# Eight stores of W2's raw blocks, issued 7 to 25 steps sooner

## The chip, the core and the metric

The kernel runs on one core of one Trainium2 chip. The metric is the time of one execution in microseconds on the device. A profiled execution gives, beside its own time, a span: first to last instruction of the core.

## What is computed

Grouped-query attention over 8 batches (16 query heads, 4 key and value heads, 384 tokens, head width 64) is followed by a ResMLP block with per-channel scales. In the reference's words, cut to what matters:

```python
attn = softmax(q @ k.T / sqrt(64));  x = heads side by side of (attn @ v)   # 8 x 384 x 1024
a1 = alpha1 * x + beta1
u  = x + lam * einsum('ts,bsd->btd', w_tok, a1)
a2 = alpha2 * u + beta2
out = u + lam * (np.maximum(a2 @ w_ch1, 0.0) @ w_ch2)    # w_ch1 1024 x 4096, w_ch2 4096 x 1024
```

The change lies in the last product, with `w_ch2`, called W2 from here.

## The kernel before

The batches are worked in four pairs. For each pair there are two large products: the first makes the hidden layer from `w_ch1`, the second multiplies it by W2. Both are done with a fast 2 x 2 scheme of seven half-size products, so that W2 is used as seven operand matrices, numbered 1 to 7: raw quarters of W2 (1, 2 and 3), and differences of quarters (4 to 7). Each operand matrix is kept as four blocks `c` of 512 KB in bfloat16.

The first pair is special. It reads W2's raw quarters from the input (float32, turned to bfloat16 on the way by transfers that GpSimd starts, L491), uses them, builds the differences with VectorE in `sum_w2` (L499), and stores each of the 28 blocks to a scratch tensor in HBM, `w2s`, with `keep_w2` (L494, started by SyncE). The other three pairs only read `w2s` back (`fetch`, L528). The blocks of one quarter carry its name: "11" lies at fixed places in the tile `arena` since the first product, "21", "12" and "22" pass through six slots of 512 KB in a ring (tile `w1`, called `w` in the profile) and three slots in the tile `pad`. "again" is the quarter "21" read a second time from `w2s` (L489).

The second product of the first pair, `second_product`, is a generator. It runs 21 turns of 16 matmuls of 128x128 by 128x512 (L752) and yields after every four, so that it has 84 steps, 0 to 83. Its turns are, as (operand, block of tokens): (1,0), (1,1), (2,0), (2,1), (1,2), (5,0), (2,2), (5,1), (5,2), then three each for operands 3, 6, 7 and 4. Operand 3 begins with step 36: its four blocks "22" 0 to 3 are read in steps 36, 37, 38 and 39.

When a slot comes free, `free` calls `pump`, which starts the next entry of one list, `queue`. The loads of "22" stand there behind those of "12": block 0 goes to `pad` at once, blocks 1 to 3 go to slots that operand 2 frees in its last turn, steps 24 to 27. The next entries are the four "again" blocks, then the blocks of `w_ch1` for the second pair (`load_w1`, L183).

Into the yields of both products other work is put by a table written out by hand, `plan`: what `put(pair, product, step, ...)` names is emitted just after that step. In the first pair's second product these are, besides the work on W2, the attention of batches 2 and 3 (`side(2)` at steps 0 to 39, `side(3)` 38 steps later): scores (L260), exponentials (L269), the product with v (L295), normalising (L303), the token product (L324 and L328), and for each pair of heads `p` a store of the sum (L227, SyncE) and a transpose by a transfer (L337, SyncE). Transposing transfers of q and k for batch 3 (L174, L170, SyncE) stand at steps 8, 14, 27, 32 and 33.

Each engine takes its instructions in the order of emission. SyncE's are nearly all starts of transfers, and in the built program each waits, beside its data, for the landing of the transfer that stands eight before it on that engine. The sums of heads lie in a pool of four buffers (`xr`) and the inputs of L337 in five places of `obuf`, so that a late store or transpose holds the buffer for the pair of heads four or five later.

Of the kernel before, what the change touches and what calls it, by code (L numbers as in the profile page):

```python
# [13 lines left out]
def kernel(  # L14
# [932 lines left out]
    with tc.manual_schedule(engines=order):  # L947
# [123 lines left out]
        def put(ps, phase, at, *m):  # L1071
            plan.setdefault((ps, phase, at), []).append(m)
# [25 lines left out]
        for c in range(4):  # L1098
            put(0, 0, (50, 72, 74, 44)[c], load_w2, "11", c)
            put(0, 0, (6, 14, 42, 46)[c], cast_w2, "21", c)  # L1100
            put(0, 1, (41, 43, 45, 47)[c], keep_w2, 1, c)
            put(0, 1, 38 + 2 * c, keep_w2, 3, c)
            put(0, 1, (9, 10, 13, 15)[c], sum_w2, 5, c)
            put(0, 1, (20, 21, 25, 26)[c], sums_first_hid, 2, c)
            put(0, 1, (28, 30, 31, 34)[c], sums_first_hid, 4, c)
            put(0, 1, (37, 40, 41, 43)[c], sum_w2, 6, c)
            put(0, 1, (44, 45, 49, 50)[c], sums_first_hid, 3, c)
            put(0, 1, (51, 54, 57, 58)[c], sum_w2, 7, c)
            put(0, 1, (61, 64, 68, 71)[c], last_w2, c)
        for u, o in ((77, 5), (79, 7), (81, 6)):  # L1110
            put(0, 1, u, sum_w1, 0, o)
        for ps in range(NB - 1):
            c = 2 * ps + 2
# [100 lines left out]
```

## Time and profile before

| | |
|---|---|
| median of 3 runs | 732.74 us (732.49 to 738.95) |
| the profiled execution's own time | 731.92 us |
| its span | 729.9 us |
| TensorE busy | 717.4 us, 98% |
| VectorE, ScalarE, GpSimd busy | 75%, 51%, 27% |
| granted TensorE clock | 1.000 |
| second product of the first pair | from 128.1 to about 234.3 us of the span |

The engines are called PE (TensorE), DVE (VectorE), ACT (ScalarE), POOL (GpSimd) and SP (SyncE) in the profile; q0 is the queue of the transfers that POOL starts, q1 that of SP's. An engine's busy time is only worth something where the end waits for that engine, so the stretch around the change is read by itself.

### The profile page before, as it was taken

To read this page: it belongs to the slowest core of one execution; us is meant where nothing else is said; L and a number is where in the kernel's file an instruction comes from. 1 tells how busy PE (TensorE), PEld (TensorE's weight loads), DVE (VectorE), ACT (ScalarE), POOL (GpSimd) and SP (SyncE) were. 2 spreads that over 40 slices of the span, in tenths; PEclk is the share of its full clock that TensorE was granted. 3 is DMA by queue.
4 is the path that set the end of the run, shared out by engine and by line. 5 is a ranking of instruction groups with operands and counts; after the bars stand their busy time and mean duration, and the time that the engine had idled before them with its cause. 6 is when DMAs were issued, how large, how long until landed. Compare 5 with 4: busy or idle time off the path is not lost.

```text
span 729.9 us, 14511 instructions
## 1 busy us (share of the span) xinstructions
PE 717.4 (98%) x5716; PEld 408.7 (56%) x5716; DVE 543.9 (75%) x1009; ACT 373.8 (51%) x566; POOL 199.2 (27%) x242
## 2 busy tenths in 40 slices
PE   8899999999999999999999999999999999999998
PEld 4665555555555666555555566655555566654444
DVE  7888876577888988649678888748868988763354
ACT  7877666544563666643433466663333366650000
POOL 8844233221046551201022344200002222000011
PEclk9999999999999999999999999999999999999999
DMA  9999999999999999969989999998989999937965
GB/s 164 180 239 231 190 195 227 226 242 235 366 312 232 179 182 196 234 221 207 272 193 220 160 162 194 212 227 201 270 233 183 210 126 146 165 123 264 302 174 104
DMA packets 197616, 153.26 MB, mean 210 GB/s; under 512 B 90540, under 2 KB 175892, under 8 KB 197292
## 3 DMA queue, kind: packets, MB, share of 16 engines
q0 software_dynamic: 109872, 64.47, 65.4%
q1 hardware_dynamic: 86988, 87.42, 42.8%
q8 instruction: 44, 0.72, 0.4%
q10 hardware_dynamic: 688, 0.46, 0.2%
q14 instruction: 24, 0.20, 0.1%
HBM read 155.23 MB, written 39.85 MB: 267 GB/s over the span
## 4 chain that ended last, share of the span: by engine, by line
PE 90%; DVE 4%; POOL 2%; DMA 1%; issue 1%; ACT 1%; DVEq 0%; ACTq 0%; POOLq 0%
PE C L897 30%; PE X L831 17%; PE C L752 10%; PE Y L831 9%; PE Z L831 4%; PE sc L260 4%; PE X L681 4%; PE sc L295 3%; PE sc L324 3%; PE Y L681 3%; DMA ops<-obuf 1%; DVE pad L565 1%; PE Z L681 1%; PE tok L324 1%; POOL obuf L334 0%
## 5 line engine op out<-in xcount | busy, mean ns | idle before, releaser
L897 PE MATMUL C<-w,arena 128*128 128x512 bf16 (+2 forms) x744 | 168.3, 372 | 0.0
L269 ACT ACTIVATE es<-sc 128x1024 bf16<-128x1024 f32 x108 | 104.1, 1024 | 116.0 <-PE sc L260 107.6
L897 PEld LDWEIGHTS <-arena 128*128 128x128 bf16 x1040 | 94.8, 98 | 100.5 <-issue 5.1
L442 POOL DMA_DIRECT2D out_dram<-hT x45 | 40.0, 888 | 294.7 <-DVE hT L790 135.9
L836 ACT ACTIVATE hT<-X,bias 128x384 f32<-128x384 f32 x144 | 83.6, 582 | 60.0 <-PE X L831 55.2
L831 PEld LDWEIGHTS <-w 128*128 128x128 bf16 x768 | 75.1, 98 | 50.0
L831 PEld LDWEIGHTS <-pad 128*128 128x128 bf16 x576 | 56.4, 98 | 37.2
L183 POOL DMA_DIRECT2D w<-in_moe_w_ch_dram x48 | 45.4, 1002 | 105.6 <-PE X L831 36.5
L831 PE MATMUL X<-ops,w 128*128 128x384 bf16 x384 | 70.3, 326 | 0.0
L831 PE MATMUL X<-ops,pad 128*128 128x384 bf16 x384 | 70.3, 326 | 0.0
L897 PE MATMUL C<-pad,arena 128*128 128x512 bf16 (+2 forms) x296 | 70.2, 373 | 0.0
L324 PEld LDWEIGHTS <-wtokT 128*128 128x128 bf16 x576 | 39.0, 98 | 16.4 <-issue 3.4
L752 PEld LDWEIGHTS <-arena 128*128 128x128 bf16 x336 | 29.8, 98 | 30.0 <-issue 2.5
L331 DVE TENSOR_TENSOR xr<-sc,xr 128x384 f32<-128x384 f32 x48 | 26.5, 553 | 25.6 <-PE sc L324 14.3
L752 PE MATMUL C<-w,arena 128*128 128x512 bf16 x168 | 41.2, 379 | 0.0
L838 DVE TENSOR_TENSOR arena<-Y,hT 128x384 bf16<-128x384 f32 x48 | 26.5, 556 | 17.7 <-ACT hT L836 16.0
L295 PEld LDWEIGHTS <-es 128*128 128x128 bf16 x864 | 32.8, 97 | 11.3
L831 PE MATMUL Y<-ops,w 128*128 128x384 bf16 x192 | 39.1, 326 | 0.0
L831 PE MATMUL Z<-ops,w 128*128 128x384 bf16 x192 | 39.0, 326 | 0.0
L269 ACT ACTIVATE hT<-sc 128x1024 bf16<-128x1024 f32 x36 | 35.8, 1031 | 4.3 <-PE sc L260 4.0
L260 PE MATMUL sc<-qT,kT 64*128 64x384 bf16 (+2 forms) x504 | 37.2, 271 | 0.5 <-ACT hT L269 0.2
L842 ACT ACTIVATE arena<-X,bias 128x384 bf16<-128x384 f32 x48 | 27.9, 582 | 17.7 <-PE X L831 16.1
(190 smaller groups left out, 1175.1 us busy)
## 6 DMA issues: line engine op xcount, KB each, us to landing
w<-w2s SPq DMA_DIRECT2D x67, 512.0 KB, 5.1
w<-in_moe_w_ch_dram POOLq DMA_DIRECT2D x65, 512.0 KB, 9.8
pad<-w2s SPq DMA_DIRECT2D x25, 512.0 KB, 6.9
out_dram<-hT POOLq DMA_DIRECT2D x45, 256.0 KB, 7.1
out_dram<-xr SPq DMA_DIRECT2D x48, 192.0 KB, 5.3
q_raw<-in_q_dram POOLq DMA_DIRECT2D x28, 192.0 KB, 9.5
w2s<-w SPq DMA_DIRECT2D x10, 512.0 KB, 7.6
arena<-in_moe_w_ch_dram POOLq DMA_DIRECT2D x8, 512.0 KB, 15.9
```

Source lines behind the costliest of these rows:

```text
L183: nc.gpsimd.dma_start(out=w1[:, w1_slots[c]], in_=w1src[:, :, c * CW * P:(c + 1) * CW * P])
L260: nc.tensor.matmul(out=sc[:, hh, k % 4:k % 4 + n], lhsT=kT_[r, 2 * p // G, BLK[hh][sk], :], rhs=qT_[r, p, st:st + n, :], start=True, stop= ...
L269: nc.scalar.activation(out=e, in_=sc, func=EXP, scale=scale_qk)
L295: nc.tensor.matmul(out=av[:, hh, sq, :], lhsT=ess[k // 4][:, m % 2, k % 4, :], rhs=vb[:, sk, hk, :], start=(sk == 0), stop=(sk == NST - 1))
L324: nc.tensor.matmul(out=ps[:, tt, :], lhsT=wtokT[:, st, tt * P:(tt + 1) * P], rhs=a1s[p][:, st, :], start=(st == 0), stop=(st == NST - 1 an ...
L442: nc.gpsimd.dma_start(out=by_tok(out[b])[:, ms, dw * 512:(dw + 1) * 512], in_=o, accum_op=ADD)
L681: nc.tensor.matmul(out=ps[:, :n], lhsT=tb[G, o][:, dt, e * P:(e + 1) * P], rhs=opb(FIRST1[o], n)[:, dt], start=(o in (1, 2, 7) and dt == 0 ...
L752: nc.tensor.matmul(out=x, lhsT=lead_hid[:, t, FIRST2[o], ms * P:(ms + 1) * P], rhs=rhs[:, t % 4 * 512:(t % 4 + 1) * 512], start=(o in (1, ...
L831: nc.tensor.matmul(out=ps, lhsT=tb[g, o][:, dt, e * P:(e + 1) * P], rhs=opb(LEFT1[o])[:, dt], start=(o in (1, 2, 7) and dt == 0), stop=(dt ...
L836: nc.scalar.activation(out=snap[o, e], in_=ps, func=IDENT, bias=hi if o == 5 else lo)
L842: nc.scalar.activation(out=hid[:, t, 4], in_=ps, func=RELU, bias=hi)
L897: nc.tensor.matmul(out=x, lhsT=hid[:, t, LEFT2[o], ms * P:(ms + 1) * P], rhs=rhs[:, t % 4 * 512 + c0:t % 4 * 512 + c1], start=((not last o ...
```

## The change

The four stores of operand 1 (the blocks "11", from `arena`) go from steps 41, 43, 45, 47 to steps 16, 18, 20, 22. The four stores of operand 3 (the blocks "22", block 0 from `pad`, 1 to 3 from the ring) go from steps 38, 40, 42, 44 to steps 24, 32, 34, 37. Nothing is added and nothing removed.

```diff
         for c in range(4):
             put(0, 0, (50, 72, 74, 44)[c], load_w2, "11", c)
             put(0, 0, (6, 14, 42, 46)[c], cast_w2, "21", c)
-            put(0, 1, (41, 43, 45, 47)[c], keep_w2, 1, c)
-            put(0, 1, 38 + 2 * c, keep_w2, 3, c)
+            put(0, 1, (16, 18, 20, 22)[c], keep_w2, 1, c)
+            put(0, 1, (24, 32, 34, 37)[c], keep_w2, 3, c)
             put(0, 1, (9, 10, 13, 15)[c], sum_w2, 5, c)
```

On PE, ACT, DVE and POOL the order of instructions stays as it was. On SP the eight stores stand earlier among the stores (L227) and transposes (L337, L174, L170) of the attention, and the loads of "again" (L489) follow the remaining stores directly.

## The prediction

> **What bounds the kernel now.** I read the page first, its busy times and the chain that ended last.
>
> ```profile
> PE 717.4 (98%) x5716; PEld 408.7 (56%) x5716; DVE 543.9 (75%) x1009; ACT 373.8 (51%) x566; POOL 199.2 (27%) x242
> PE 90%; DVE 4%; POOL 2%; DMA 1%; issue 1%; ACT 1%; DVEq 0%; ACTq 0%; POOLq 0%
> ```
>
> TensorE is busy for 717.4 of 729.9 us, and the chain is PE for 90%. A store can therefore only matter by making PE wait, or by ending a wait that PE has now. So next I read the busy times by stretch over the second product of the first pair (columns: PE, PEld, DVE, ACT, POOL, granted clock, DMA share, GB/s).
>
> ```profile
> 127.00:152.00 25.00, 25.00 (x232) 13.77 (x231) 16.43 (x28) 12.59 (x16) 8.20 (x8) 1.00 1.24 249
> 152.00:178.00 26.00, 26.00 (x254) 14.46 (x253) 18.62 (x31) 13.90 (x18) 4.95 (x5) 1.00 1.09 206
> 178.00:206.00 28.00, 27.41 (x264) 15.42 (x261) 22.72 (x35) 17.11 (x26) 0.91 (x1) 1.00 1.04 351
> 206.00:234.00 28.00, 26.81 (x249) 15.03 (x248) 25.42 (x40) 13.56 (x22) 16.00 (x15) 1.00 1.16 276
> ```
>
> The reader is to see two things. PE has no gap at all up to 178 us and only 0.59 + 1.19 = 1.8 us of gaps after it: that is all the change could win here. And the stores stand now in the stretch from 178 to 206 us, with 351 GB/s; they go to the stretch before, which shows 206 GB/s but a DMA share just as full (1.09): slower traffic, not free engines.
>
> Third, the order of time on PE, for the moments at which operand 3 takes its blocks "22" 1, 2 and 3 (the first line holds two blocks), and the landings of their three loads, each asked for by itself.
>
> ```profile
> 174.33 1.89 PE L752 MATMUL C<-w,arena 128*128 128x512 bf16 x8
> 176.91 1.04 PE L752 MATMUL C<-w,arena 128*128 128x512 bf16 x4
> ```
>
> ```profile
> L491 POOL DMA_DIRECT2D w<-in_moe_w_ch_dram x1: 782/782/782, 158.5 to 158.5; - x1
> DMA to landing us min/median/max: 5.8/5.8/5.8
> ...
> L491 POOL DMA_DIRECT2D w<-in_moe_w_ch_dram x1: 766/766/766, 159.9 to 159.9; - x1
> DMA to landing us min/median/max: 9.6/9.6/9.6
> ...
> DMA to landing us min/median/max: 9.6/11.2/12.8
> ```
>
> The third load is issued at 160.7 us, behind the second (the last line holds both), and takes 12.8 us. So the blocks land at 164.3, 169.5 and 173.5 us. PE wants them at 174.33, at about 175.2 (four matmuls of 0.22 us later) and at 176.91. The margins are 10.0, 5.7 and **3.4 us**. The last is the smallest cushion in the stretch, and the moved stores are put right in front of it.
>
> Fourth, the DMA queues in two windows of 2 us, 162 to 164 (first line) and 166 to 168 (the other two): the loads of "22" alone, and beside one 512 KB transfer of SP's.
>
> ```profile
> q0 software_dynamic: 372, 0.36, 117.6%
> ...
> q1 hardware_dynamic: 103, 0.42, 57.5%
> q0 software_dynamic: 183, 0.17, 52.8%
> ```
>
> q0 falls from 0.36 to 0.17 MB per 2 us while q1 moves 0.42 MB. So SP's transfers take their time from POOL's loads.
>
> **The change, part by part.**
>
> *The store instructions.* Eight starts leave SP's stretch from 179.3 to 199 us and enter that from 155 to 182. A store's start has a median of 1.01 us from `arena`, 0.70 from `pad` and 0.45 from `w`. PE never waits for a start, so as work they cost nothing.
>
> *What they pass on SP.* I place them by SP's order of time: the store and transpose of head pair 1 end at 154.9. Then comes "11" 0 (to 156); head pair 2, now at 155.4 to 157.4, ends at 157.8; "11" 1 to 3 take three starts of 1.0 (to 160.8); head pair 3 is issued at about 161 instead of 157.44; "22" 0 follows at 163, then the load "again" 0 (now 162.2), head pair 4, the transpose of q, and "22" 1 at about 171. "22" 2 comes before head pair 6, "22" 3 after it. What is late next: the buffer of head pair 3's store is wanted by DVE at 173.22 (L303, head pair 7). Stores of this kind take 3.4 to 8.9 us to land in this product, so issued at 161 it lands by 170. Head pair 4's buffer is wanted only at 182.2. The transposes of q and k that are passed serve scores from 202 us on. I cost all this at 0; if the cover of 3 us at head pair 3 is gone, DVE and through it the token product of head pair 7 (PE, 177.78) wait by what is over.
>
> *New waits on SP.* "22" 1 waits for its load (landed 164.3, or some us later), with head pair 5, the transposes of k and q and "22" 2 queued behind it. SP gets there at about 171, so the wait is 0. "22" 3 waits for the load that PE itself wants at 176.91, and behind it are head pair 7's store and transpose and the stores of operand 6, whose buffers are wanted after 187. Cost 0, with cover of some 5 us.
>
> *The bytes.* This is the price. One 512 KB store (0.524 MB) beside the loads costs q0 0.19 MB x 0.524 / 0.42 = 0.24 MB, and at its own 0.18 MB/us that is 1.3 us of delay. The loads' packets run from 160 to about 172. "11" 0 is gone by then. Of "11" 1 a half, "11" 2 and 3 and "22" 0 fall into it: 3.5 stores, 4.6 us. The third block then lands at 178.1 and **PE waits 1.2 us at step 39**. The second lands at 174.1, 1.1 us ahead of its use. Bounds: if only two stores meet the loads (2.6 us), 176.1 is in time and the cost is 0; if five do ("11" 1 to 3, "22" 0 and 1), 6.5 us give 180.0 and a wait of 3.1 us. I take 3.5, as the starts on SP fall.
>
> *What is taken away later.* Between 184 and 200 us q1 is full, and the loads and stores there go faster without the eight. These waits end with it:
>
> ```profile
> 204.10 1.23 DVE L499 TENSOR_TENSOR arena<-pad,arena 128x2048 bf16<-128x2048 bf16 x1 [1.10 <-DMA w2s<-arena]
> 198.28 0.91 POOL L183 DMA_DIRECT2D w<-in_moe_w_ch_dram x1 [31.03 <-PE sc L328]
> ```
>
> DVE waits 1.10 us for a store of "11" before it overwrites the block, and the first load of `w_ch1` starts at 198.28 only, though PE read the last block of its slot at 187.4: the store of "22" 3, issued at 191.24, still held it. But DVE's next work on the chain, L331 at 205.85, needs a PE result of 205.5 and would not start sooner; PE's gap at 204.89 (0.59 us) was ended by an exponential on ACT, that at 224.76 (0.95 us) by DVE work that came after idle time of DVE; and the `w_ch1` block is used after 229 us. Value 0, with a bound of -1.8 us, all gaps of PE here.
>
> **Sum.** 731.92 us (the profiled execution's own time, 2.0 over its span) + 1.2 - 0 = 733.1. The median of the runs shown is 0.82 above that execution, so I forecast 732.74 + 1.2 = **733.9 us**, a loss of 0.2%. Its own range is 732.5 to 735.8 (0 to 3.1 us of wait).
>
> **The rivals.**
>
> *Nothing (732.7).* The load is late by less than 3.4 us, or SP gets its stores out so late, behind head pairs 2 and 3, that they follow the loads. For it: the loads hold their own queue, and 2.6 us of delay is the lower bound. Against: SP issues one transfer after another at 155 to 161, so the stores are not late.
>
> *Faster (731.0 to 732.4).* The gaps after 178 us shrink as traffic leaves 184 to 200 us, and the load of "22" keeps its margin. For it: the 1.10 us of DVE. Against: none of PE's gaps ends with a transfer. It decides when the delay of "22" 3 is below 3.4 us and DVE's wait is upstream of the gap at 204.89.
>
> *Much slower (741.4): equal turns.* In the window from 203 to 211 us, where SP has steady work, the queues stood so:
>
> ```profile
> q1 hardware_dynamic: 1202, 1.86, 70.4%
> q0 software_dynamic: 1037, 0.52, 47.5%
> ```
>
> That is nearly packet for packet, and q0 gets 0.065 MB/us. At that rate the three loads (1.57 MB) last 24.2 us from 160; with 1.4 us from the last packet to the landing (the first load's 0.52 MB at 0.18 MB/us from 160 is through at 162.9 and landed at 164.3) block 3 lands at 185.6, PE waits 8.7 us, and the time is 741.4. It decides once SP's work lasts until the loads are through. Against it: the stores that can come in time are some 2.6 MB, or 11 us at the 0.23 MB/us of that window; and the packets of q0 there were half as large (0.50 KB; from 162 to 164 they are 0.97 KB).
>
> [...]
>
> **How the numbers follow.** The short wait has a chance of 0.57, nothing 0.20, faster 0.08, equal turns 0.15. All but the last lie within 1% of 732.74 (7.3 us; 1% is about what a measurement of this kernel can tell from no change): PE's gaps cap any gain at 1.8 us, so over 1% faster gets 0.02 for what I do not see, slower by over 1% gets 0.13 (some of the last case stays below it), and 0.85 is left. The range is 731.8 to 737.5: the forecast's own with its upper bound widened for equal turns that end early, the whole of "nothing" and half of "faster".
>
> **What would show it.** In the profile after: "22" 3 landing at about 178 instead of 173.5, and an idle time of about 1 us on PE in front of the L752 group now at 176.91; SP's "11" 1 to 3 issued from 157 to 161; no wait of DVE for `w2s<-arena` at 204; the first L183 near 188; and q1 well under 6.0 MB from 184 to 200. A PE without a gap before 180 proves the delay wrong in size, and a gap over 4 us the equal turns right. A PE gap at 173 to 178 that ends with L303 or L324 would mean that the passed stores, not the bytes, were the price.

## The result, and the profile after

| | before | after |
|---|---|---|
| median of 21 runs each | 732.92 us | 736.93 us |
| ratio after to before | | **1.0049**, 95% interval 1.003 to 1.0068 |
| the profiled execution's own time | 731.92 us | 733.94 us |
| its span | 729.9 us | 732.2 us |
| runs with a mean granted clock of 0.998 or less | 18 of 105 (beside the experiments) | 17 of 21 |

The kernel became slower, by 0.5% in the median and by 2.0 us (0.3%) between the two profiled executions, both of which show a clock of 1.000. The busy times and the chain that ended last, on the page of the changed kernel:

```profile
PE 718.5 (98%) x5716; PEld 409.3 (56%) x5716; DVE 544.8 (74%) x1009; ACT 373.6 (51%) x566; POOL 198.3 (27%) x242
PE 78%; DMA 7%; issue 5%; DVE 5%; POOL 4%; ACT 1%; SPq 0%; POOLq 0%; DVEq 0%; ACTq 0%
```

The work is the same; DMA's share of the chain went from 1% to 7%, mostly because the chain now runs through a load of W2 (`w<-in_moe_w_ch_dram`, 5% by itself). The busy times by stretch (PE, PEld, DVE, ACT, POOL, granted clock, DMA share, GB/s) say where:

```profile
152.00:178.00 26.00, 24.52 (x244) 13.71 (x242) 18.20 (x30) 14.24 (x19) 4.94 (x5) 1.00 1.12 274
178.00:206.00 28.00, 27.38 (x253) 15.15 (x253) 22.16 (x34) 15.09 (x23) 0.91 (x1) 1.00 1.08 304
```

In the stretch up to 178 us, where PE had no gap, 1.48 us of idle time appear; the traffic there rose from 206 to 274 GB/s at a DMA share that was full before (1.09, now 1.12). PE's order of time over this product (last column: idle time before the group, and what ended it) names the wait:

```profile
173.86 1.89 PE L752 MATMUL C<-w,arena 128*128 128x512 bf16 x8
...
178.59 1.02 PE L752 MATMUL C<-w,arena 128*128 128x512 bf16 x4 [2.07 <-DMA w<-in_moe_w_ch_dram]
...
206.56 0.33 PE L324 MATMUL sc<-a,wtokT 128*128 128x128 bf16 x3 [0.59 <-ACT es L269]
...
222.87 0.33 PE L398 MATMUL sc<-ident,obuf 128*128 128x128 bf16 x3 [0.24 <-ACT es L269]
...
226.43 0.34 PE L324 MATMUL sc<-a,wtokT 128*128 128x128 bf16 x3 [0.95 <-DVE a L309]
```

The first line holds the reads of "22" 1 and 2, both in time; the second is that of "22" 3, which waits **2.07 us** for its load. The three gaps after it were all there before the change, with the same sizes and the same releasers. The load itself, asked for alone:

```profile
L491 POOL DMA_DIRECT2D w<-in_moe_w_ch_dram x1: 740/740/740, 160.3 to 160.3; - x1
...
DMA to landing us min/median/max: 18.3/18.3/18.3
```

It was issued at 160.3 and landed at 178.6 instead of 173.5. And the queues from 160 to 174 us (packets, MB, share of 16 engines), first in the kernel before, then in the changed one:

```profile
q0 software_dynamic: 1724, 1.83, 84.2%
q1 hardware_dynamic: 1283, 0.90, 29.9%
```

```profile
q1 hardware_dynamic: 1511, 2.83, 61.8%
q0 software_dynamic: 1178, 1.17, 51.2%
```

q1 carries 1.93 MB more and q0, the loads, 0.66 MB less. On SP, in order of time (start, length):

```profile
154.13 0.34 SPq L494 DMA_DIRECT2D w2s<-arena  x1
...
156.63 1.90 SPq L494 DMA_DIRECT2D w2s<-arena  x3
...
161.37 0.58 SPq L494 DMA_DIRECT2D w2s<-pad  x1
162.05 0.48 SPq L489 DMA_DIRECT2D w<-w2s  x1
...
167.39 8.18 SPq L174 DMA_TRANSPOSE qT<-q_raw  x1
175.66 0.54 SPq L494 DMA_DIRECT2D w2s<-w  x1
```

The four stores of "11" and the first of "22" have been started before 162 us. The transposing transfer of q then holds SP for 8.18 us, so "22" 1 starts only at 175.66.

### The profile page after: what moved, and what is told of

Same layout as the page of the kernel before. It is cut to its first block, busy times and chain, and to the rows that moved or that the text cites. A ratio compares the mean times of both kernels' runs of the same rounds, so it can differ in the third digit from the quotient of the medians.

```text
span 732.2 us, 14511 instructions
## 1 busy us (share of the span) xinstructions
PE 718.5 (98%) x5716; PEld 409.3 (56%) x5716; DVE 544.8 (74%) x1009; ACT 373.6 (51%) x566; POOL 198.3 (27%) x242
## 4 chain that ended last, share of the span: by engine, by line
PE 78%; DMA 7%; issue 5%; DVE 5%; POOL 4%; ACT 1%; SPq 0%; POOLq 0%; DVEq 0%; ACTq 0%
PE C L897 30%; PE X L831 13%; PE Y L831 7%; DMA w<-in_moe_w_ch_dram 5%; PE sc L260 4%; PE X L681 4%; PE Z L831 3%; PE C L752 3%; PE Y L681 3%; PE sc L295 3%; PE sc L324 2%; POOL hT L790 2%; DMA out_dram<-xr 1%; PE E L613 1%; PE av L295 1%
## 5 line engine op out<-in xcount | busy, mean ns | idle before, releaser
L324 PEld LDWEIGHTS <-wtokT 128*128 128x128 bf16 x576 | 39.0, 98 | 16.3 <-issue 3.4
```

What stands on the lines that cost most here:

```text
L324: nc.tensor.matmul(out=ps[:, tt, :], lhsT=wtokT[:, st, tt * P:(tt + 1) * P], rhs=a1s[p][:, st, :], start=(st == 0), stop=(st == NST - 1 an ...
```

## The experiments

The theory to be tested: the bytes of SP's transfers, those of "11" above all, slow the loads of "22". Its rivals: the place of the stores in SP's order is the price (what is queued behind them), or the transposes; and for the size, what lies beyond the 2 us of wait. Edits are against the kernel before unless it says "changed kernel". "Ratio" is against the kernel before, run on the same chip beside it.

**The two halves.** `again` is the changed kernel a second time.

```diff
 # only1: "11" moved alone
+put(0, 1, (16, 18, 20, 22)[c], keep_w2, 1, c)
 put(0, 1, 38 + 2 * c, keep_w2, 3, c)
 # only3: "22" moved alone
 put(0, 1, (41, 43, 45, 47)[c], keep_w2, 1, c)
+put(0, 1, (24, 32, 34, 37)[c], keep_w2, 3, c)
```

> The changed kernel once more, for a second profile: its profiled execution (733.94 us, PE wait 2.07 us at step 39, clock 1.000) lies below the median of 736.93 us, and most of its runs show a mean granted clock of 0.997 or less. Theory A (the stores' bytes delay the loads of "22"; how long varies from run to run): the profile shows a wait for w<-in_moe_w_ch_dram at step 39 of 2 to 5 us, and if the clock is under 1.000, the lower clock lies right behind that wait. Rival C (the rest of the loss has another place): a clock under 1.000 lies elsewhere, with the wait at step 39 again near 2 us. Ratio 1.003 to 1.007 by both.

> Only the four stores of "11" are moved (steps 16 to 22). Theory A: three of the four meet the loads of "22", 3 x 1.4 us = 4.2 us of delay against a margin of 3.4, so PE waits about 0.8 us (0 to 2) at step 39 and the ratio is 1.000 to 1.003. Rival B (what delays the loads is not the stores' bytes but the transposes that the stores push back into the loads' time, above all the one of q that took 8.18 us at 167.39): the transposes of head pairs 2 and 3 are pushed back just as in the full change, so the wait is 2 us or more and the ratio 1.004 to 1.006.

> Only the four stores of "22" are moved (steps 24, 32, 34, 37). Theory A: one store, block 0, meets the loads, 1.4 us of delay, under the margin of 3.4: no wait at step 39, ratio 0.999 to 1.001. Rival B: the transposes behind it are pushed back by one start, some 1 us; also no wait. Rival D (SP held by a store that waits for its load, with head pairs 5 to 7 queued behind it): PE or DVE waits at head pairs 5 to 7 between 170 and 200 us, ratio over 1.002.

| | ratio (95%) | wait at step 39 | "22" 3 lands after | q0 / q1, 160 to 174 us |
|---|---|---|---|---|
| again | 1.0037 (1.0021 to 1.0053) | 1.95 us | 18.2 us | 1.13 / 2.84 MB |
| only1 | 1.005 (1.0025 to 1.0075) | 2.45 us | 18.7 us | 1.19 / 2.55 MB |
| only3 | 1.0042 (1.0015 to 1.0069) | 0 | 14.3 us | 1.71 / 1.37 MB |

PE's order of time in `only1`, the same group as above:

```profile
178.94 1.02 PE L752 MATMUL C<-w,arena 128*128 128x512 bf16 x3 [2.45 <-DMA w<-in_moe_w_ch_dram]
```

The stores of "11" alone make the whole wait. It is larger than expected of the bytes (0.8 us, at most 2), and by its size and its ratio `only1` fits rival B, the transposes that are pushed back, as well; `tiny` below decides between the two. The stores of "22" alone leave step 39 in time and still cost 4.2 us of span (734.1 against 729.9), which the expectation did not have. Where, the order of time on POOL, on DVE and on PE in `only3` shows:

```profile
187.23 0.91 POOL L183 DMA_DIRECT2D w<-in_moe_w_ch_dram  x1 [20.67 <-PE C L752]
```

```profile
200.12 1.22 DVE L499 TENSOR_TENSOR arena<-w,arena 128x2048 bf16<-128x2048 bf16 x1 [3.01 <-DMA w2s<-arena]
...
205.54 1.23 DVE L499 TENSOR_TENSOR arena<-pad,arena 128x2048 bf16<-128x2048 bf16 x1 [1.25 <-DMA w2s<-arena]
...
208.53 1.23 DVE L499 TENSOR_TENSOR arena<-pad,arena 128x2048 bf16<-128x2048 bf16 x1 [1.77 <-DMA w2s<-arena]
```

```profile
209.81 1.02 PE L752 MATMUL C<-arena 128*128 128x512 bf16 x4 [1.36 <-DVE arena L499]
...
228.95 0.34 PE L324 MATMUL sc<-a,wtokT 128*128 128x128 bf16 x3 [1.66 <-DVE a L309]
```

With "22" 3 stored early, its slot is free early, and the first load of `w_ch1` starts at 187.23 instead of 198.28: beside the stores of "11", which in this kernel are still on their way. They land late, DVE waits 6.0 us for them before it overwrites the blocks, and PE loses it in pieces. PE's gaps from 202 to 229 us add up to 5.9 us, against 1.8 before.

**Bytes or order.** `tiny` puts starts with few bytes where the changed kernel has the stores of "11": 64 of the 2048 columns there, the rest at the old steps. `dose2` moves two of the four.

```diff
 # tiny: keep_part stores columns lo to hi of block c
+put(0, 1, (16, 18, 20, 22)[c], keep_part, c, 0, 64)
+put(0, 1, (41, 43, 45, 47)[c], keep_part, c, 64, 2048)
 put(0, 1, 38 + 2 * c, keep_w2, 3, c)
 # dose2 and dose2b
+put(0, 1, (16, 18, 45, 47)[c], keep_w2, 1, c)
 put(0, 1, 38 + 2 * c, keep_w2, 3, c)
```

> SP's order of the moved "11" stores without their bytes: at steps 16 to 22 each of the four stores carries 64 of a block's 2048 columns, and the other 1984 follow at the old steps 41 to 47; the stores of "22" stay at 38 to 44. Theory A (bytes): the loads of "22" land as before the change (block 3 about 13 us after its issue), no wait at step 39, ratio 0.999 to 1.002. Rival B/C (the order on SP: four more starts, each waiting for the transfer eight before it, push back the transposes and the stores of head pairs 2 to 4): the wait of 2.0 to 2.5 us at step 39 stays, ratio 1.003 to 1.006.

> Only "11" 0 and 1 are moved, to steps 16 and 18; the other six stores stay where they were. Theory A: at most two stores meet the loads, 2 x 1.5 = 3.0 us of delay against a margin of 3.4: block 3 lands 14 to 16 us after its issue, no wait at step 39 (0 to 0.5 us), ratio 1.000 to 1.002, and the granted clock stays at 0.999 or more. Rival (any store in front of the loads costs the full wait, because SP's queue as a whole is behind): 2 us as with four stores.

> Once more only "11" 0 and 1 at steps 16 and 18, since the first profile of it showed an execution far from its own median. Theory A: in a profile near 732 to 734 us the loads of "22" move some 1.4 to 1.5 MB between 160 and 174 us (1.83 before the change, 1.17 after it), block 3 lands 14 to 16 us after its issue, and PE waits 0 to 0.5 us at step 39. Rival (all or nothing): 1.2 MB, 18 us and 2 us of wait.

`tiny`, to be held against `only1`: ratio 1.002 (0.9992 to 1.0048), no wait at step 39, "22" 3 lands after 14.3 us. The same order of starts on SP with a thirty-second of the bytes gives no wait there. (It is not a clean pair: in this profile PE is some 2 us later than in the others and SP's small stores start at 158.84 and from 161.32, up to 4 us later than in `only1`. Further on the rest of "11" goes out late, and DVE waits 5.2 us for it, as in `only3`.)

`dose2`: ratio 1.0014 (0.9977 to 1.0052). Its profile fell on an execution of 743.66 us, 9.8 above its own median. In that execution the wait is there, and larger than in the changed kernel, with two stores only:

```profile
179.33 1.02 PE L752 MATMUL C<-w,arena 128*128 128x512 bf16 x4 [2.28 <-DMA w<-in_moe_w_ch_dram]
...
184.71 1.02 PE L752 MATMUL C<-w,arena 128*128 128x512 bf16 x3 [3.59 <-DMA w<-in_moe_w_ch_dram]
```

"22" 3 lands there just before 184.71, where PE's second wait ends on it. `dose2b` is the same kernel again, with a profile of 732.09 us, near the medians of both (733.90 and 732.93): ratio 0.9978 (0.9935 to 1.0021), no wait at step 39, landing after 15.1 us. The queues in `dose2b` from 160 to 174 us:

```profile
q0 software_dynamic: 1485, 1.49, 66.0%
q1 hardware_dynamic: 2379, 1.88, 53.2%
```

So from none over two to four stores of "11" moved, q1 in that window goes 0.90, 1.88, 2.55 MB (`only1`), q0 1.83, 1.49, 1.19 MB, and the landing 12.8, 15.1, 18.7 us. In this execution two stores take 2.3 of the 3.4 us of cushion and cost no wait; four take more than there is. With `tiny` this makes the bytes the cause. How late the block lands differs more from one execution to another than these profiles alone would say, as that of `dose2` shows.

**Less around the loads.** `noagain` lets the load "again" 0, which SP starts at 162.05 in the changed kernel, wait behind "again" 1. `noflip` takes the transposes of q and k that stood at steps 27, 32 and 33 to 41, 42 and 43. `calm` is the kernel before with the edit of `noagain`.

```diff
 # noagain: changed kernel; calm: kernel before
-("again", (0,), w1_free), ("again", (1,), pad_free), ("again", (2, 3), w1_free)
+("again", (1,), pad_free), ("again", (0, 2, 3), w1_free)
 # noflip: changed kernel
-zip((8, 14, 14, 27, 32, 33)
+zip((8, 14, 14, 41, 42, 43)
```

> The full change, but the load of "again" 0, 512 KB that SP starts at about 162 us beside the loads of "22", comes behind "again" 1 in the queue, near 190 us. Theory A: any 512 KB of SP's that leaves the loads' time gives back about 1.4 us, so the wait at step 39 falls from 2.0 to about 0.6 us (0 to 1.2) and the ratio to 1.000 to 1.003. Rival B (the transposes are what delays): they only move forward on SP, the wait stays at 2 us or grows.

> The full change, with the three transposes of q and k of steps 27, 32 and 33 moved to steps 41, 42 and 43, so that none of them stands in the loads' time (one took 8.18 us of SP at 167.39). Theory A (bytes of the stores first, what follows on SP second): the delay is made by the four stores before 168 us; the wait at step 39 falls by no more than 1.3 us, to 0.7 to 2.0 us. Rival B (the transposes are what delays the loads): block 3 lands within 15 us of its issue and the wait is gone. In both cases the transposes now share the stretch after 178 us with the stores, which can cost PE at scores (202 us) if they land late; ratio 1.000 to 1.005.

> The kernel before with one edit: the load of "again" 0 (512 KB on SP's queue at 162 us, beside the loads of "22") goes behind "again" 1, near 190 us. Theory A: the loads of "22" keep more of the engines, block 3 lands about 1.3 us earlier (11.5 us after its issue instead of 12.8), the margin at step 39 grows from 3.4 to about 4.7 us; the median stays (ratio 0.998 to 1.001), and fewer runs should show a granted clock under 0.999, if those come from a wait at step 39. Rival: transfers that follow on SP move up and take the same time: landing unchanged, ratio 1.000, clocks as before. The risk is the other side: "again" 0 then shares the stretch after 184 us with the stores of "11" (VectorE's wait of 1.10 us at 204 grows), ratio up to 1.003.

| | ratio (95%) | wait at step 39 | "22" 3 lands after | q0 / q1, 160 to 174 us |
|---|---|---|---|---|
| noagain | 1.0013 (0.9989 to 1.0037) | 1.93 us | 18.1 us | 1.22 / 2.47 MB |
| noflip | 1.0029 (0.9987 to 1.0071) | 2.90 us | 19.1 us | 1.20 / 2.44 MB |
| calm | 0.9994 (0.9957 to 1.0031) | 0 | 11.8 us | 1.84 / 1.10 MB |

Neither brought the wait down, though 0.6 us had been expected of `noagain` and 0.7 to 2.0 of `noflip`. In `noagain` q1 moves 0.36 MB less than in the changed kernel, but the landing is only 0.2 us sooner. What it loses in bytes it makes up in packets, of which the view shows 1737 in the window for 1511. So it does not hold that any 512 KB less gives back 1.4 us. The wait stays (1.93 us); whether its time is nearer to before than that of `again` the intervals leave open. In `noflip` it grows: where the transpose of q stood, SP now starts "22" 1 (at 168.71 for 175.66), and from 172 to 176 us the queues show

```profile
q1 hardware_dynamic: 293, 0.93, 63.1%
q0 software_dynamic: 307, 0.31, 45.9%
```

against these in the changed kernel:

```profile
q0 software_dynamic: 425, 0.42, 61.9%
q1 hardware_dynamic: 422, 0.68, 52.6%
```

In both the two queues show nearly as many packets, one of q0 to one of q1. But a packet of q1 has 0.93 / 293 MB = 3.2 KB in the one and 1.6 KB in the other; fewer packets pass in the 4 us (600 for 847), and the load gets 0.31 MB instead of 0.42. By these sizes a transpose looks the better neighbour of a load: from 164 to 168 us of the changed kernel, where SP is in its transposes, q1's packets have 0.27 MB / 564 = 0.5 KB, and the loads get 0.56 MB. No run tests this by itself. `calm`, where SP has no such queue, lands the block 1 us sooner than before, but its time isn't told apart from no change.

**Other places.** `early1` puts "11" at the start of the product, `late1` four steps later than the change, and `only3hold` repairs `only3` by leaving the store of "22" 3 at its old step.

```diff
 # early1
+put(0, 1, 2 * c, keep_w2, 1, c)
 put(0, 1, 38 + 2 * c, keep_w2, 3, c)
 # late1: changed kernel
-put(0, 1, (16, 18, 20, 22)[c], keep_w2, 1, c)
+put(0, 1, (20, 22, 24, 26)[c], keep_w2, 1, c)
 # only3hold: "11" at its old steps
+put(0, 1, (24, 32, 34, 44)[c], keep_w2, 3, c)
```

> The stores of "11" are moved further ahead, to steps 0, 2, 4 and 6, and those of "22" stay at 38 to 44: the bytes go out at 128 to 140 us, where SP's queue is nearly empty, and none meets the loads of "22". Theory A: no wait at step 39, landing of block 3 near 173.5; the loads of "12" land up to 5 us later than now, VectorE's differences for operand 5 (140 to 148 us) may wait up to 1 us, PE does not; ratio 0.999 to 1.001. If the relief of the stretch from 182 to 200 us were worth something, the ratio would be 0.998 or less. Rival B gives the same at step 39, since no transpose is pushed back.

> The full change, but the stores of "11" at steps 20, 22, 24 and 26, so that all four stand beside the loads of "22" and none goes out ahead of them. Theory A: one store more in the loads' time, wait at step 39 of 3 to 4.5 us instead of 2.0; ratio 1.005 to 1.010. On the clock: if it is the single long idle time of PE that lowers the granted clock in many runs of the changed kernel (0.992 to 0.998, against 0.999 and 1.000 in nearly all runs of before), it must show here in most runs, and in the profile right behind the wait; if the lower clock has nothing to do with the wait, its share of the runs stays near half.

> Like the run with only the "22" stores moved, but block 3's store stays at its old step 44 (24, 32, 34, 44), so that its slot, and with it the first load of w_ch1 (L183), is held until about 198 us as before. Theory: in the run with all four, the load of w_ch1, which then started at 187 us, took the engines from the stores of "11", VectorE waited 6.0 us for these and PE lost 4.8 us in five gaps from 202 to 229. Held back, these gaps go: VectorE's wait for w2s<-arena is 2 us or less in all, ratio 0.999 to 1.002. Rival (order on SP: the "22" stores in front push the "11" stores back by themselves): VectorE's wait stays at 4 us or more and the ratio at 1.003 to 1.006.

`early1`: ratio 1.0047 (1.002 to 1.0074), where no change had been expected. Step 39 is in time, but the same thing happens to the loads of "12". DVE's and PE's order of time:

```profile
144.59 1.78 DVE L499 TENSOR_TENSOR w<-w,arena 128x2048 bf16<-128x2048 bf16 x1 [1.44 <-DMA w<-in_moe_w_ch_dram]
```

```profile
147.13 0.39 PE L260 MATMUL sc<-qT,kT 64*128 64x128 bf16 x4 [2.39 <-DVE xr L303]
```

q0 moves 0.88 MB from 128 to 140 us there, against 2.08 before; DVE waits for blocks of "12" (0.54, 1.44 and 0.21 us), and PE for a result of DVE's that is queued behind them.

`late1`: ratio 1.005 (1.0029 to 1.0072). The landing takes 19.8 us, and PE waits twice, for "22" 2 and "22" 3, 3.42 us in all (3 to 4.5 had been expected):

```profile
176.05 1.02 PE L752 MATMUL C<-w,arena 128*128 128x512 bf16 x4 [0.88 <-DMA w<-in_moe_w_ch_dram]
...
180.38 1.07 PE L752 MATMUL C<-w,arena 128*128 128x512 bf16 x3 [2.54 <-DMA w<-in_moe_w_ch_dram]
```

`only3hold`: ratio 0.9997 (0.9955 to 1.004). `w_ch1` starts at 199.11 again, DVE waits 1.6 us where `only3` had 6.0, and the loss is gone. So it was the early store of "22" 3, by the slot that it frees early, and not the other three stores, that cost `only3` its 4 us.

**The clock.** In `late1` and `noflip` the profiled executions have a mean clock of 0.997. `late1` from 178 to 186 us (columns as in the stretches above; the granted clock is the third from the end):

```profile
178.00:180.00 2.00, 0.00 (x0) 0.00 (x0) 0.00 (x0) 2.00 (x3) 0.00 (x0) 1.00 1.28 186
180.00:182.00 2.00, 1.57 (x11) 1.14 (x12) 0.00 (x0) 0.81 (x2) 0.00 (x0) 0.80 1.29 118
182.00:184.00 2.00, 2.00 (x11) 1.13 (x10) 1.20 (x3) 0.66 (x2) 0.00 (x0) 0.50 1.09 386
184.00:186.00 2.00, 2.00 (x10) 0.79 (x8) 2.00 (x2) 0.00 (x0) 0.00 (x0) 0.84 1.29 315
```

Right behind the wait the clock falls to half: 2 us x (0.20 + 0.50 + 0.16) = 1.72 us are lost on top of the wait. With the two waits (3.42 us) this makes up the 5.1 us by which the span is longer than before (735.0 for 729.9). In `noflip`, behind 2.90 us, the same four windows show 0.95, 0.50, 0.70 and 1.00, which is 1.70 us. In the first profile of `dose2`, behind 3.59 us, the three windows from 184 to 190 us show 0.95, 0.50 and 0.70, again 1.70 us.

## Why the prediction was right, and where its terms were off

**The bytes: right as the cause, and near in size.** The step "3.5 stores meet the loads" gave 4.6 us and a landing at 178.1; it was 5.5 us (18.3 for 12.8) and 178.6. `only1`, `dose2b` and `tiny` show that it is the bytes. The price of one store, put at 1.3 us from a single window of 2 us, is by the 0.98 MB that `dose2b` adds to q1 (1.87 stores) 2.3 / 1.87 = 1.2 us, and by the 1.93 MB of the changed kernel (3.7 stores) 5.5 / 3.7 = 1.5 us. It is no constant: in `only3` and `only3hold` 0.47 and 0.48 MB more on q1 go with a landing 1.5 and 2.5 us later, and in `noagain` 0.36 MB less brought 0.2 us.

**The wait: its mechanism right, its size 2.07 us for 1.2.** Of the 0.9 us of difference, half is the later landing (0.5 us); the other half is that PE reached step 39 at 176.5 in this execution, 0.4 us sooner than in the one before (173.86 for 174.33). Against the profiled execution the sum holds: 731.92 + 2.07 = 734.0, and 733.94 was measured.

**The clock: the term that the sum did not have.** The median rose by 4.0 us, about twice the wait. At 736.93 it lies above the short wait's own range (732.5 to 735.8). It lies within the stated range only because that was widened upward for equal turns that end early, and in neither profile is the wait longer than 2.07 us. That much of the hit is luck. The two profiled executions of the changed kernel (clock 1.000, and 0.999 in `again`) show only the wait, at a clock of 1.00 around it. But 17 of its 21 runs have a clock of 0.998 or less, with a median of 737.1 us; the four at 1.000 have 734.1, which is before plus 1.2. The same split appears in `again` (6 of 12; 737.5 against 734.9). `late1` and `noflip` show what such a loss looks like, 1.7 us right behind the wait. Over the experiments, the kernels whose profile shows the wait at step 39 (`again`, `only1`, `noagain`, `noflip`, `late1`) have a clock of 0.998 or less in 31 of 59 runs, those whose profile does not (`only3`, `early1`, `tiny`, `dose2b`, `calm`, `only3hold`) in 12 of 70. But `noagain`, with 1.93 us of wait, has it in 3 of 12 only. That those runs of the changed kernel lose the time at step 39 is argued from this, not shown: no profile caught one of them. The first profile of `dose2` shows that one execution can have a later landing and a longer wait than the rest, and the lower clock behind it. The prediction took PE's idle time as the whole cost of it.

**The starts that are passed, cost 0: right.** No wait on L303 or L324 appeared before step 39. SP's starts came sooner than forecast up to "22" 0: three stores of "11" took 1.90 us together, not 1.0 each, head pair 3 started at 158.62 (161 forecast) and "22" 0 at 161.37 (163). "22" 1 came late, at 175.66 instead of about 171, because the transpose of q took 8.18 us on SP. It cost nothing here: `noflip`, with the store in the place of that transpose, waited longer.

**What is taken away later, value 0: right, for a reason that the text lacked.** DVE's 1.10 us at 204 is gone (the two additions stand as one unbroken group at 203.45) and PE's gaps are the same three: the rival "faster" falls. The first load of `w_ch1` came at 190.35, near the 188 forecast, and q1 moved 4.11 MB from 184 to 200 for 6.00. But an early `w_ch1` load is harmless here because the stores of "11" have left by then: with them at their old place it costs 4 us (`only3`).

**Equal turns: the counts came, the price did not.** From 164 to 176 us the queues of the changed kernel stand so:

```profile
q0 software_dynamic: 1383, 1.38, 69.9%
q1 hardware_dynamic: 1386, 1.51, 47.7%
```

That is one packet of q0 to one of q1, as in `noflip` above (307 to 293), and as equal turns would have it; the view counts packets and does not show their order. What was wrong is the rival's rate, taken from a window in which q0's packets had 0.50 KB. The packets of these loads have 1.0 KB, and q0 gets 1.38 / 12 = 0.115 MB/us instead of 0.065. With that rate, and q0's first packets at 162.7, the rival's own working gives 162.7 + 1.57 / 0.115 + 1.4 = 177.8; measured was 178.6. (The rate is that of the same loads, so this only shows that the working closes.) So the forecast, with a price from one window of 2 us, came near the size without the counts, and the rival had the counts with a rate that did not fit. In windows of 4 us with equal counts the loads got 0.56 MB beside packets of 0.5 KB on q1, 0.42 beside 1.6 KB and 0.31 beside 3.2 KB.

**What neither had: the late first packet.** In the kernel before q0's first packets of these loads run at 160.0, 1.5 us after the first issue. In the changed kernel, from 160 to 162 us, the view of the queues holds only one:

```profile
q1 hardware_dynamic: 220, 0.79, 96.8%
```

q0's first come at about 162.7, 4.7 us after an issue at 158.0. So 3.2 of the 5.5 us (4.7 for 1.5 behind the issue) are gone before both queues have packets, while the engines work through stores started by 158.5. In `only1` q0 moves 0.11 MB from 160 to 164 us, where it moves 0.59 in the kernel before and 0.07 in the changed one. In `dose2b` its first packets come after 162.0, at least 3.9 us behind an issue at 158.1, and that accounts in the same way for all of the 2.3 us. The step "3.5 stores meet the loads" thus had the amount about right and the manner only in part: in the changed kernel and in `dose2b` more than half of the delay comes from stores that stand in front of the loads, and the rest falls into the time in which both queues have packets. The kernel before shows the same with the parts exchanged: SP starts "again" 0 at 162.20, while the engines work through the loads, and the queues hold no packet of q1 from 162 to 165.5 (q0 at 118.7% there). Why the later transfer shows no packets at first, the runs don't say.

**What else the runs say of the change.** The old steps, 38 to 47, lie between two deadlines: sooner, the stores meet the loads of "22" (or of "12"); with other traffic beside them, DVE waits to overwrite "11" (6.0 us in `only3`, 5.2 in `tiny`). That it would wait longer if they came later is likely from the 1.10 us before, but no run tries it. No kernel run here is shown to be faster than the one before; the three nearest, `dose2b`, `only3hold` and `calm`, can't be told from it. Open is why the kernel before shows the lower clock in 18 of 105 runs (median 739.1, against 732.9 of those at 1.000): none of those was profiled.

## What to carry to other kernels

Ask of a store that is moved which load it will share the DMA engines with, how large the packets of both are, and how much cushion the load has: here 2 stores of 512 KB fitted into 3.4 us in one profile and not in another, and 4 did not. A cushion that is nearly used up can be gone in a single execution (`dose2`, waits of 2.28 and 3.59 us, for none in `dose2b`). A stretch with less traffic in GB/s is not a free stretch where its DMA share is already full (here 206 GB/s at 1.09). Where one queue has a backlog, taking one transfer out of it can move the next one up rather than make room (`noflip`: "22" 1 started at 168.71 for 175.66, and PE waited 2.90 us for 2.07), and a slot freed early starts the next load early (`only3`: at 187.23 for 198.28), which can then be the one that disturbs.

## What the runs showed of the hardware

The granted clock fell behind the longest waits of PE. In the profiles of `again`, of the changed kernel and of `only1`, waits of 1.95, 2.07 and 2.45 us left it at 1.00; in those of `late1`, `noflip` and `dose2`, 2.54, 2.90 and 3.59 us brought it to 0.50 in one window of 2 us, for 1.7 us of loss each, and it was back at 1.00 from 186, 184 and 190 us on. That is no measured threshold between 2.45 and 2.54 us: the wait in `late1` followed another, of 0.88 us, as that in `dose2` followed one of 2.28 us, behind which the clock had stayed at 1.00. How long PE must be idle for it, these runs don't show.

The two queues showed nearly as many packets as each other in several windows in which both had work. From 164 to 176 us q0 and q1 show 1383 to 1386 packets in the changed kernel, 1255 to 1252 in `only1`, 1237 to 1224 in `noflip` and 962 to 956 in `late1`; the kernel before shows 507 to 497 from 168 to 172 us, but 183 to 103 from 166 to 168. And a load issued into a backlog of stores had no packet for 4.7 us, a transfer of SP's issued into a backlog of loads none for 3.3 us.

The start of the transposing transfer of q (L174) behind head pair 4 took SP 8.18 us in the changed kernel and 4.51 us in the one before. It took 8.47 us in `again` and 6.72 in `only1`, where four whole stores of "11" had been started from step 16 on as well, and 4.44, 5.18 and 3.28 us in `only3`, `early1` and `tiny`, where not; those of L337 from 152 to 182 us took 1.2 to 6.5 us in these runs and in `noflip`. So a long start went with the traffic of those stores ahead of it, and it decided when the transfers behind it began: in the changed kernel "22" 1 at 175.66, in the one before the store behind the transpose at 170.07.
